# Stores issued by GpSimd, more buffers for divided weights and words, g written into other tiles, and the operands of x made in the order of their products

## The chip, the cores and the metric

The kernel runs on one core of a Trainium2 chip. A core has five engines that run side by side: TensorE (PE, matmuls; PEld is its weight load), VectorE (DVE), ScalarE (ACT), GpSimd (POOL) and SyncE (SP, which here only issues DMAs). Each engine takes its instructions strictly in the order in which the program lists them, and waits on semaphores for the others. The metric is the device time of one execution in microseconds (us), lower is better; the numbers below are for one core and one program.

## What is computed

Attention with a sigmoid in place of the softmax, over 8 batches, 12 heads, 448 tokens and 64 columns a head, then a bilinear feed-forward layer on the 3584 x 768 result:

```
scores = q @ k.T / sqrt(64) - log(448)
x      = concat_heads(sigmoid(scores) @ v)      # 3584 x 768
h      = ((x @ w1) * (x @ w2)) @ w3             # 3584 x 1024
out    = h @ w_out                              # 3584 x 768
```

The four weights are of type float64 and reach the kernel as pairs of 32-bit words. The kernel makes float32 values of them itself ("decode").

## The kernel before, in words

**Precision.** A float32 operand is divided into a high part in the type `fp32r` and the rest, also in that type: `split` casts the high part (`h...`, on ACT or DVE) and lets DVE subtract it (`l...`). A product is three matmuls: high x high, high x low, low x high.

**Products.** `x @ w` is done with Strassen's scheme in Winograd's form: seven products instead of eight. The two batches 2g and 2g+1 are one group g (four groups). For each of the three 128-wide slices kc of x, seven operands are made of the four blocks A11, A12, A21, A22 of x: A11, S2, A12, S3, S1, A22, S4, in the order of the products (`PRODUCTS`). S1 = A21 + A22, S2 = S1 - A11, S3 = A11 - A21, S4 = A12 - S2. `up(g)` runs over the eight 128-wide slices fc of the hidden width and, in each, over the seven products k; a product is 9 matmuls (3 slices kc x 3). After each product ACT (`p`, `c11`) or DVE (`u2`, `u3`, `c22`) takes its sum out of the accumulators; after k = 5 and k = 6 DVE multiplies two of these tiles and the result g goes to DRAM (`g_dram`).

**Weights.** `prepare_weights` decodes w1 and w2 slice by slice (12 steps on DVE for each fc, plus a magnitude on ACT), and `finish_weights` makes the seven weight operands of a slice, divides each of them (`divide`: a cast on ACT, a subtraction on DVE, tile `wo`) and stores it (`w_dram`). `load_weights` fetches them again for each group into a ring of six tiles `w`. `prepare_rest` does the same decoding for w3 and w_out (tiles `raw` and `f`, 32 jobs).

**Order.** All engines follow the order in which the program is written. Attention is a row of 168 items, two to a burst k (84 bursts and one more); a burst issues the scores of its two items, the sigmoids on ACT, and the products with v of the burst before. From burst 25 on, `up(0)` is taken between attention (504 matmuls over bursts 25 to 52, 18 a burst), then `up(1)` (bursts 58 to 66, 56 a burst) and `up(2)` (71 to 79). `up(3)` follows the last burst. After each product `beside` takes steps of other streams: one step of `change` (the operands of x for the next group, from `groups`), else 3 or 4 steps of `weights` in group 0, else 2 steps of `rest`. In bursts without products four steps of `change` and two of `weights` are taken. In group 0 the operands are made in `combine`, as soon as a slice of x is there.

**Queues.** Before the change every DMA is issued by SP, in program order: loads of `qk`, `vv`, `raw` and `w`, and the stores of `wo`, `f` and g. `finish_weights` keeps the stores of two divided weights back (`made`), with three buffers `wo`; `up` keeps the stores of g until the next product.

**The end.** Under the last matmuls of `up(3)` w_out is loaded and split (`woh`, `wol`, eight slices) and the first two slices of w3 (`w3`, `w3h`, `w3l`); then w3 @ w_out (L702) and the last product (L827) follow, which the change does not touch.

Of the kernel before, what the change touches and what calls it, by code (L numbers as in the profile page):

```python
# [25 lines left out]
def sigmoid_attention_bilinear_ffn(  # L26
# [20 lines left out]
    P = 128  # L47
# [168 lines left out]
    def early(g, kc):  # L216

        for name in ("A11", "S3"):
            split_operand(g, name, kc, xf[g, name, kc])
            yield  # L220

    def late(g, kc):

        a11, a12, s1, a22 = (xf.pop((g, name, kc)) for name in ("A11", "A12", "A21", "A22"))
        split_operand(g, "S1", kc, s1)
        yield
        total(a11, s1, a11, ALU.subtract)
        split_operand(g, "S2", kc, a11)
        yield
        if g > 0:  # L230
            split_operand(g, "A12", kc, a12)
            yield
        total(a12, a12, a11, ALU.subtract)
        split_operand(g, "S4", kc, a12)
        yield
        split_operand(g, "A22", kc, a22)
        yield

    def combine(n, acc):
# [53 lines left out]
    def finish_weights(fc, fs):  # L293

        b11, b21, b12, b22 = (f[:, h * KH:(h + 1) * KH] for f in fs for h in range(2))
        made = []
# [7 lines left out]
        def store():  # L304
            k, wo = made.pop(0)
            nc.sync.dma_start(out=w_dram[fc * 7 + k], in_=wo.bitcast(F32))
# [19 lines left out]
        n4 = subtract("n4", b21, t2)  # L326
# [4 lines left out]
        store()  # L331
        yield 1
        store()

    RING = 6
    stored = set()
# [16 lines left out]
            jobs.append((src, wo_dram[ic, :, ms]))  # L353
    def prepare_rest():

        def load(i):
            return load_words(jobs[i][0], p2[0]) if i < len(jobs) else None

        raw = [load(0), load(1)]
        yield  # L360
        yield
        f = magnitude(raw[0], p2[0], 3)
        store = None
        for i, (_, dst) in enumerate(jobs):
            for step, _ in enumerate(decode(raw[i % 2], f)):
                if step == 0 and store:
                    nc.sync.dma_start(out=store[0], in_=store[1])
# [6 lines left out]
        nc.sync.dma_start(out=store[0], in_=store[1])  # L374
        yield

    def up(g):

        at = {b: slice(b * S, (b + 1) * S) for b in (2 * g, 2 * g + 1)}
        stores = []  # L380
        for fc in range(NF):
            tags = ["up0", "up1"] * 2 if g < NG - 1 else ["up0", "up1", "av", "av"]
            if fc % 2 and g < NG - 1:
# [13 lines left out]
            def add(out, a, b):  # L397
                nc.vector.tensor_tensor(out=out, in0=a, in1=b, op=ALU.add)  # L398

            def leave(b, a, out):  # L400
                nc.vector.tensor_tensor(out=out, in0=a, in1=out, op=ALU.mult)
                stores.append((g_dram[fc, :, at[b]], out))

            for k, name in enumerate(PRODUCTS):
                n = (g * NF + fc) * 7 + k
                load_weights(n + RING - 1)
                w = ring.pop(n)
                while any((name, kc) not in ops[g] for kc in range(KH)):
                    next(change)
                for dst, src in stores:  # L410
                    nc.sync.dma_start(out=dst, in_=src)
                stores.clear()
                bank, start, stop = ((0, 1, 0), (1, 1, 0), (0, 0, 1), (1, 0, 1),
                                     (2, 1, 0), (3, 1, 1), (2, 0, 1))[k]
                if start:
                    chain(bank)
                a = acc[bank]
                for kc in range(KH):
                    xh, xl = ops[g][name, kc]
                    for m, (i, x) in enumerate(((0, xh), (0, xl), (1, xh))):  # L420
                        nc.tensor.matmul(  # L421
                            a, w[:, i, kc], x, start=bool(start) and kc == 0 and m == 0,
                            stop=bool(stop) and kc == KH - 1 and m == 2, skip_group_check=True,
                        )
                        if (kc, m) != (KH - 1, 2):
                            yield
# [6 lines left out]
                elif k == 2:  # L433
                    c11 = kept("c11")
                    nc.scalar.copy(out=c11, in_=a)
# [12 lines left out]
                beside(g, n)  # L448
                yield
        for dst, src in stores:  # L450
            nc.sync.dma_start(out=dst, in_=src)

    def take(stream, n):
        done = 0
# [9 lines left out]
    zeros = p1.tile([P, 512], F32R, name="wo", bufs=3)  # L464
    nc.vector.memset(zeros.bitcast(F32), 0.0)

    def idle_products(n):
# [27 lines left out]
    def groups(g):  # L495
        if g < NG - 1:
            for kc in range(KH):
                yield from early(g, kc)
                yield from late(g, kc)
            return  # L500
        for kc in range(KH):
            yield from early(g, kc)
        for kc in range(KH):
            while (g, "A22", kc) not in xf:
                yield
            yield from late(g, kc)

    qks, splits, vvs = {}, {}, {}
    qks[0] = load_pair(0)
# [46 lines left out]
    for k in range(NBURST + 1):  # L556
# [43 lines left out]
    phase_a.close()  # L600
# [261 lines left out]
```

## Time and profile before

| | |
|---|---|
| time, median of 3 runs | 1085.17 us (1083.5 to 1087.89) |
| the profiled execution, its own time | 1085.67 us |
| the profiled execution, span of its trace | 1083.8 us |
| PE busy | 1004.1 us of the span |
| mean granted TensorE clock | 0.962 |
| DVE, ACT busy | 650.3 us, 410.7 us |
| DMA | 226.39 MB, mean 209 GB/s |

Busy times are sums over the span. A row of the waits reads: the waiting engine, its tile and line, who ended the wait; total us, number of waits, the longest. A row of the timeline reads: start, length, engine, line, operation, tiles, and in brackets the idle time before it with what ended it. A row of the stages reads: from:to, length, then busy us and number of instructions of PE, PEld, DVE, ACT and POOL, the granted clock, the DMA engines' busy share and GB/s.

### The profile page before, as it was taken

The page shows a single profiled execution, that of the slowest core. Times are in us where ns is not written, and L with a number is a line of the kernel's source. Part 1 is how long each engine was busy: PE and PEld are TensorE (multiplying, and loading weights), DVE is VectorE, ACT ScalarE, POOL GpSimd, SP SyncE. Part 2 cuts the span into 40 slices and gives each one's busy share as a digit, 9 for nine tenths or more (in the row PEclk, how much of TensorE's full clock was granted, in tenths as well). Part 3 has the DMA queues.
Part 4 walks back from the last instruction along what each step waited for, and adds up shares of the span by engine and source line. Part 5 has one row for each costly group of instructions (what it writes and reads, how often), then busy time and mean ns, then how long its engine had stood idle before and what let it go on. Part 6 is the DMA issues. An engine that isn't in the chain of part 4 may idle for free.

```text
span 1083.8 us, 14159 instructions
## 1 busy us (share of the span) xinstructions
PE 1004.1 (93%) x5250; PEld 766.4 (71%) x5250; DVE 650.3 (60%) x1042; ACT 410.7 (38%) x598; POOL 0.2 (0%) x4
## 2 busy tenths in 40 slices
PE   9976879888999899999799999799989999999998
PEld 4432456555666487777377777499879999999997
DVE  5767456766733966667856674844335565666563
ACT  6855634444553632323523332411114342323130
POOL 0000000000000000000000000000000000000000
PEclk9987989888999999999899999899999999999999
DMA  7554587787975487899387896098834113433402
GB/s 240 195 186 163 200 310 265 282 278 264 329 266 178 125 299 245 300 329 323 102 285 259 309 314 216 17 323 296 287 129 166 55 59 112 161 106 133 135 36 77
DMA packets 122436, 226.39 MB, mean 209 GB/s; under 512 B 10752, under 2 KB 80384, under 8 KB 122368
## 3 DMA queue, kind: packets, MB, share of 16 engines
q1 hardware_dynamic: 122368, 225.49, 61.6%
q8 instruction: 42, 0.69, 0.3%
q14 instruction: 26, 0.21, 0.1%
HBM read 170.39 MB, written 55.05 MB: 208 GB/s over the span
## 4 chain that ended last, share of the span: by engine, by line
PE 50%; DVE 5%; DMA 1%; ACT 1%; issue 1%; SPq 0%; DVEq 0%; ACTq 0%
PE up L421 21%; PE up L827 19%; PE up L702 6%; PE av L189 1%; PE sp L166 1%; DMA w<-w_dram 1%; DVE lS L67 1%; DVE A L214 1%; DVE lA L67 1%; DVE u L398 0%; PE sp L176 0%; DVE hS L66 0%; PE av L197 0%; ACT a L156 0%; DVE low L67 0%
## 5 line engine op out<-in xcount | busy, mean ns | idle before, releaser
L421 PE MATMUL up<-hS,w 128*128 128x448 f32 x768 | 244.2, 377 | 30.0 <-DVE u L398 13.1
L827 PE MATMUL up<-gh,wo 128*128 128x448 f32 x672 | 192.2, 367 | 0.0
L421 PEld LDWEIGHTS up<-hS,w 128*128 128x128 f32 x768 | 146.7, 192 | 64.1 <-DVE u L398 14.6
L156 ACT ACTIVATE a<-sp,bias 128x896 f32<-128x896 f32 x168 | 160.5, 1004 | 75.7 <-PE sp L166 71.5
L421 PE MATMUL up<-hA,w 128*128 128x448 f32 x576 | 183.6, 372 | 3.4 <-ACT p L429 3.2
L421 PE MATMUL up<-lS,w 128*128 128x448 f32 x384 | 143.2, 373 | 0.3 <-DVE lS L67 0.2
L827 PEld LDWEIGHTS up<-gh,wo 128*128 128x128 f32 x672 | 126.1, 188 | 11.3
L189 PE MATMUL av<-a,vv 128*64 128x448 f32 x576 | 132.5, 575 | 0.0
L421 PEld LDWEIGHTS up<-hA,w 128*128 128x128 f32 x576 | 109.5, 190 | 25.5 <-issue 7.8
L827 PE MATMUL up<-gl,wo 128*128 128x448 f32 x336 | 123.2, 367 | 0.0
L421 PE MATMUL up<-lA,w 128*128 128x448 f32 x288 | 106.7, 371 | 0.0
L166 PE MATMUL sp<-high 64*128 64x448 f32 x288 | 65.9, 454 | 37.9 <-ACT a L156 37.8
L398 DVE TENSOR_TENSOR u<-up,p 128x448 f32<-128x448 f32 x64 | 39.9, 623 | 83.5 <-PE up L421 78.6
L166 PEld LDWEIGHTS sp<-high 64*128 64x128 f32 x288 | 28.9, 197 | 85.7 <-ACT a L156 60.4
L189 PEld LDWEIGHTS av<-a,vv 128*64 128x64 f32 x576 | 35.0, 141 | 68.5 <-issue 67.3
L76 ACT ACTIVATE f<-raw 128x768 f32<-128x768 f32 (+2 forms) x48 | 34.5, 720 | 121.1 <-DMA raw<-w3T 43.9
L421 PEld LDWEIGHTS up<-lS,w 128*128 128x128 f32 x384 | 73.8, 192 | 8.3 <-issue 1.4
L827 PEld LDWEIGHTS up<-gl,wo 128*128 128x128 f32 x336 | 63.1, 188 | 5.6
L398 DVE TENSOR_TENSOR u<-up,u 128x448 f32<-128x448 f32 x64 | 39.8, 622 | 42.4 <-PE up L421 41.7
L67 DVE TENSOR_TENSOR low<-qk,high 128x896 fp32r<-128x896 f32 x48 | 52.3, 1090 | 20.2 <-ACT high L66 16.1
L421 PEld LDWEIGHTS up<-lA,w 128*128 128x128 f32 x288 | 54.8, 190 | 7.1 <-issue 2.8
L67 DVE TENSOR_TENSOR gl<-gf,gh 128x896 fp32r<-128x896 f32 x40 | 41.9, 1087 | 29.7 <-ACT gh L66 21.4
(80 smaller groups left out, 1203.1 us busy)
## 6 DMA issues: line engine op xcount, KB each, us to landing
w<-w_dram SPq DMA_DIRECT2D x224, 384.0 KB, 4.9
w_dram<-wo SPq DMA_DIRECT2D x56, 384.0 KB, 5.1
g_dram<-c SPq DMA_DIRECT2D x64, 224.0 KB, 4.0
gf<-g_dram SPq DMA_DIRECT2D x16, 896.0 KB, 5.3
raw<-w SPq DMA_DIRECT2D x16, 768.0 KB, 5.5
qk<-qT SPq DMA_DIRECT2D x48, 224.0 KB, 5.0
qk<-kT SPq DMA_DIRECT2D x48, 224.0 KB, 5.0
out<-o_sb SPq DMA_DIRECT2D x48, 224.0 KB, 2.0
```

The lines of the kernel that those rows point to most:

```text
L67: lo_engine.tensor_tensor(out=dst_lo, in0=src, in1=dst_hi, op=ALU.subtract)
L76: nc.scalar.activation(f, raw[..., 1].bitcast(F32), AF.Abs, scale=HW_SCALE)
L156: nc.scalar.activation(dst, src, AF.Sigmoid, bias=bias[:n], scale=scale)
L166: nc.tensor.matmul(sp[:, j], k[rows, 1, at:at + P], q[rows, 0], start=m == 0, stop=m == 2)
L189: nc.tensor.matmul(acc[cols, :S], vv[:, c, at:at + D], a[:, j], start=u == 0 and c == 0, stop=u == 1 and c == NC - 2,)
L214: nc.vector.tensor_tensor(out=out, in0=in0, in1=in1, op=op)
L398: nc.vector.tensor_tensor(out=out, in0=a, in1=b, op=ALU.add)
L421: nc.tensor.matmul(a, w[:, i, kc], x, start=bool(start) and kc == 0 and m == 0, stop=bool(stop) and kc == KH - 1 and m == 2, skip_group_ch ...
L702: nc.tensor.matmul(acc, a[:, jc], w[:, jc, ms], start=(jc == 0 and m == 0), stop=(jc == NF - 1 and m == 2),)
L827: nc.tensor.matmul(acc, w[:, fc, ms], g[:, fc], start=start and fc == 0 and m == 0, stop=fc == NH - 1 and m == 2, skip_group_check=True,)
```

## The change

Five parts:

1. Every store (`wo`, g, and the `f` of w3 and w_out) is issued by GpSimd at once, no longer by SP and no longer kept back. SP issues loads and the final outputs.
2. `wo` has four buffers instead of three, `raw` in `prepare_rest` four instead of two, with words loaded three jobs ahead; the magnitude of the next job is taken at step 4 instead of 2. The divisions of a slice come in the order 0, 2, 5, 1, 3, 4, 6 instead of 0, 2, 1, 3, 4, 5, 6; n4 is written over b21.
3. g is written into `u3` (k = 5) and into a new tile under the name `c22` (k = 6), instead of into `c22` and `c11`.
4. The operands of x: in group 0 the high parts of S1 to S4 are cast on DVE (all were on ACT), in the other groups those of S2 and S4 (it alternated). `groups` makes them in the order of the products over all slices kc, and a product waits slice by slice. Bursts without products take three steps of `change` instead of four.
5. Before the end, the first seven products of `up(3)` are placed ahead of the closing of the attention pools, and w3's first two slices are loaded before the eight splits of w_out instead of after them.

```diff
-        turn = g > 0 and len(ops[g]) % 2
+        turn = name in (("S1", "S2", "S3", "S4") if g == 0 else ("S2", "S4"))
...
+    def second(g, kc):
+        a11, s1 = xf.pop((g, "A11", kc)), xf[g, "A21", kc]
+        total(a11, s1, a11, ALU.subtract)
+        xf[g, "S2", kc] = a11
+        split_operand(g, "S2", kc, a11)
+
+    def fourth(g, kc):
+        a12 = xf.pop((g, "A12", kc))
+        total(a12, a12, xf.pop((g, "S2", kc)), ALU.subtract)
+        split_operand(g, "S4", kc, a12)
...
-        def divide(k, src):
-            if len(made) > 1:
-                store()
-            wo = p1.tile([P, 2, KH, P], F32R, name="wo", bufs=3)
-            split(wo[:, 0], wo[:, 1], src, nc.scalar.copy, nc.vector)
-            made.append((k, wo))
+        def divide(k, src):
+            wo = p1.tile([P, 2, KH, P], F32R, name="wo", bufs=4)
+            split(wo[:, 0], wo[:, 1], src, nc.scalar.copy, nc.vector)
+            nc.gpsimd.dma_start(out=w_dram[fc * 7 + k], in_=wo.bitcast(F32))
+            stored.add(fc * 7 + k)
...
-        for k, src in ((1, t2), (3, t3), (4, t1), (5, n4), (6, b22)):
+        for k, src in ((5, n4), (1, t2), (3, t3), (4, t1), (6, b22)):
...
-            return load_words(jobs[i][0], p2[0]) if i < len(jobs) else None
+            if i < len(jobs):
+                raw[i] = load_words(jobs[i][0], p2[0], 4)
...
-                if step == 2 and i + 1 < len(jobs):
-                    following = magnitude(raw[(i + 1) % 2], p2[0], 3)
+                if step == 4 and i + 1 < len(jobs):
+                    following = magnitude(raw[i + 1], p2[0], 3)
                 yield
-            store = dst, f
-            raw[i % 2] = load(i + 2)
+            nc.gpsimd.dma_start(out=dst, in_=f)
             f = following
...
-            def leave(b, a, out):
-                nc.vector.tensor_tensor(out=out, in0=a, in1=out, op=ALU.mult)
-                stores.append((g_dram[fc, :, at[b]], out))
+            def leave(b, a, c, out):
+                nc.vector.tensor_tensor(out=out, in0=a, in1=c, op=ALU.mult)
+                nc.gpsimd.dma_start(out=g_dram[fc, :, at[b]], in_=out)
...
-                while any((name, kc) not in ops[g] for kc in range(KH)):
-                    next(change)
...
+                    while (name, kc) not in ops[g]:
+                        next(change)
...
-                    leave(2 * g + 1, u3, c22)
+                    leave(2 * g + 1, u3, c22, u3)
...
-                    leave(2 * g, u2, c11)
+                    leave(2 * g, u2, c11, kept("c22"))
...
             for kc in range(KH):
                 yield from early(g, kc)
-                yield from late(g, kc)
+                split_operand(g, "S1", kc, xf[g, "A21", kc])
+                yield
+                second(g, kc)
+                yield
+            for name in ("A12", "A22"):
+                for kc in range(KH):
+                    split_operand(g, name, kc, xf[g, name, kc])
+                    yield
+            for kc in range(KH):
+                fourth(g, kc)
+                yield
             return
...
-            take(change, 4)
+            take(change, 3)
...
+    take(filler, 7 * KH * 3 - 9)
     take(rest, 10 ** 6)
...
+    load_w3(0)
+    load_w3(1)
     for jc in range(NF):
-        take(filler, 50)
+        take(filler, 42)
...
-    load_w3(0)
-    load_w3(1)
+    take(filler, 20)
     split_w3(0)
```

Three places show how instructions move. The first is the queue of SP around the start of `up(0)`, before the change: `w` are the loads of divided weights for coming products, `wo` the stores of weights just divided.

```order
L344 DMA w<-w_dram 128x768 x5
L306 DMA w_dram<-wo 128x768 x2
L139 DMA vv<-vL 128x3x256
L145 DMA vs<-vL 64x128 x2
L344 DMA w<-w_dram 128x768
L71 DMA raw<-w 128x6x256
L306 DMA w_dram<-wo 128x768 x2
L344 DMA w<-w_dram 128x768
L306 DMA w_dram<-wo 128x768 x2
L344 DMA w<-w_dram 128x768
```

The same place on SP now:

```order
L339 DMA w<-w_dram 128x768 x5
L71 DMA raw<-w 128x6x256
L139 DMA vv<-vL 128x3x256
L145 DMA vs<-vL 64x128 x2
L339 DMA w<-w_dram 128x768 x3
L71 DMA raw<-w 128x6x256
L339 DMA w<-w_dram 128x768
```

And the queue of POOL, which had no DMA before, from its first store on:

```order
L311 DMA w_dram<-wo 128x768 x16
L395 DMA g_dram<-u_1202 128x448
L311 DMA w_dram<-wo 128x768
L395 DMA g_dram<-c_1326 128x448
L311 DMA w_dram<-wo 128x768 x6
```

The stores have left SP's queue, where they stood between the loads, and stand alone on POOL's.

The second place is DVE around burst 18, where the first slice of x of group 0 is complete. Before, S1 (`A_605`), S2 (`A_218`) and S4 (`A_391`) were each formed (L214) and their low parts subtracted (L67) on DVE, with the cast between the two on ACT:

```order
L214 TENSOR_TENSOR A_605<-A_605,A_792 128x448
L67 TENSOR_TENSOR lS_796<-A_605,hS_795 128x448
L214 TENSOR_TENSOR A_218<-A_605,A_218 128x448
L67 TENSOR_TENSOR lS_801<-A_218,hS_800 128x448
L214 TENSOR_TENSOR A_391<-A_391,A_218 128x448
L67 TENSOR_TENSOR lS_806<-A_391,hS_805 128x448
```

Now (the tiles have other numbers):

```order
L214 TENSOR_TENSOR A_606<-A_606,A_792 128x448
L66 CAST hS_795<-A_606 128x448
L67 TENSOR_TENSOR lS_796<-A_606,hS_795 128x448
L214 TENSOR_TENSOR A_218<-A_606,A_218 128x448
L66 CAST hS_800<-A_218 128x448
L67 TENSOR_TENSOR lS_801<-A_218,hS_800 128x448
L214 TENSOR_TENSOR A_392<-A_392,A_218 128x448
L66 CAST hS_805<-A_392 128x448
L67 TENSOR_TENSOR lS_806<-A_392,hS_805 128x448
```

The three casts have joined DVE's queue and left ACT's.

The third place is DVE in the first slice of `up(3)`. Before, nearly all operands stood ahead of the sum of the second product (`u_6116`); these are the last rows ahead of it, and what follows up to the last sum:

```order
L214 TENSOR_TENSOR A_5115<-A_5115,A_4603 128x448
L66 CAST hS_6088<-A_5115 128x448
L67 TENSOR_TENSOR lS_6089<-A_5115,hS_6088 128x448
L398 TENSOR_TENSOR u_6116<-up,p 128x448
L67 TENSOR_TENSOR lA_6119<-A_6071,hA_6118 128x448
L398 TENSOR_TENSOR u_6146<-up,p 128x448
L398 TENSOR_TENSOR c_6160<-up,u_6146 128x448
L398 TENSOR_TENSOR u_6146<-up,u_6146 128x448
L401 TENSOR_TENSOR c_6160<-u_6146,c_6160 128x448
```

Now the rows from the sum of the sixth product (`u_6127`) to the sum of the seventh (`u_6093`):

```order
L391 TENSOR_TENSOR u_6127<-up,u_6127 128x448
L394 TENSOR_TENSOR u_6127<-u_6127,c_6145 128x448
L214 TENSOR_TENSOR A_4623<-A_4623,A_4224 128x448
L66 CAST hS_6167<-A_4623 128x448
L67 TENSOR_TENSOR lS_6168<-A_4623,hS_6167 128x448
L214 TENSOR_TENSOR A_4815<-A_4815,A_4497 128x448
L66 CAST hS_6177<-A_4815 128x448
L67 TENSOR_TENSOR lS_6178<-A_4815,hS_6177 128x448
L214 TENSOR_TENSOR A_5094<-A_5094,A_4580 128x448
L66 CAST hS_6185<-A_5094 128x448
L67 TENSOR_TENSOR lS_6186<-A_5094,hS_6185 128x448
L391 TENSOR_TENSOR u_6093<-up,u_6093 128x448
```

The making of S4, which the seventh product multiplies, has moved from ahead of the second product's sum to behind the sixth product's.

More of the change, by code (lines that the diff above doesn't have):

```diff
@@ L220, in early @@
             yield
+    def second(g, kc):
[7 more added lines that the diff above has]
+        split_operand(g, "S4", kc, a12)
     def late(g, kc):
-        a11, a12, s1, a22 = (xf.pop((g, name, kc)) for name in ("A11", "A12", "A21", "A22"))
-        split_operand(g, "S1", kc, s1)
+        split_operand(g, "S1", kc, xf[g, "A21", kc])
         yield
-        total(a11, s1, a11, ALU.subtract)
-        split_operand(g, "S2", kc, a11)
+        second(g, kc)
         yield
[L230 to L234, printed above, removed]
+        fourth(g, kc)
         yield
-        split_operand(g, "A22", kc, a22)
+        split_operand(g, "A22", kc, xf[g, "A22", kc])
         yield
@@ L295, in finish_weights @@
         b11, b21, b12, b22 = (f[:, h * KH:(h + 1) * KH] for f in fs for h in range(2))
-        made = []
         def subtract(name, in0, in1, out=None):
@@ L325, in finish_weights @@
         yield 1
-        n4 = subtract("n4", b21, t2)
+        n4 = subtract("n4", b21, t2, b21)
         yield 1
-        for k, src in ((1, t2), (3, t3), (4, t1), (5, n4), (6, b22)):
+        for k, src in ((5, n4), (1, t2), (3, t3), (4, t1), (6, b22)):
             divide(k, src)
             yield 1
-        store()
-        yield 1
-        store()
     RING = 6
@@ L354, in prepare_rest @@
     def prepare_rest():
+        raw = {}
         def load(i):
-            return load_words(jobs[i][0], p2[0]) if i < len(jobs) else None
-        raw = [load(0), load(1)]
-        yield
-        yield
+            if i < len(jobs):
+                raw[i] = load_words(jobs[i][0], p2[0], 4)
+        for i in range(3):
+            load(i)
+        for _ in range(6):
+            yield
         f = magnitude(raw[0], p2[0], 3)
-        store = None
         for i, (_, dst) in enumerate(jobs):
-            for step, _ in enumerate(decode(raw[i % 2], f)):
-                if step == 0 and store:
-                    nc.sync.dma_start(out=store[0], in_=store[1])
-                if step == 2 and i + 1 < len(jobs):
-                    following = magnitude(raw[(i + 1) % 2], p2[0], 3)
+            load(i + 3)
+            for step, _ in enumerate(decode(raw.pop(i), f)):
+                if step == 4 and i + 1 < len(jobs):
+                    following = magnitude(raw[i + 1], p2[0], 3)
                 yield
-            store = dst, f
-            raw[i % 2] = load(i + 2)
+            nc.gpsimd.dma_start(out=dst, in_=f)
             f = following
-        nc.sync.dma_start(out=store[0], in_=store[1])
-        yield
     def up(g):
         at = {b: slice(b * S, (b + 1) * S) for b in (2 * g, 2 * g + 1)}
-        stores = []
         for fc in range(NF):
@@ L407, in up @@
                 w = ring.pop(n)
-                while any((name, kc) not in ops[g] for kc in range(KH)):
-                    next(change)
-                for dst, src in stores:
-                    nc.sync.dma_start(out=dst, in_=src)
-                stores.clear()
                 bank, start, stop = ((0, 1, 0), (1, 1, 0), (0, 0, 1), (1, 0, 1),
@@ L443, in up @@
                     add(u3, a, u3)
-                    leave(2 * g + 1, u3, c22)
+                    leave(2 * g + 1, u3, c22, u3)
                 else:
                     add(u2, a, u2)
-                    leave(2 * g, u2, c11)
+                    leave(2 * g, u2, c11, kept("c22"))
                 beside(g, n)
                 yield
-        for dst, src in stores:
-            nc.sync.dma_start(out=dst, in_=src)
     def take(stream, n):
@@ L463, in sigmoid_attention_bilinear_ffn @@
     order.enter_context(tc.manual_schedule(engines=ALL))
-    zeros = p1.tile([P, 512], F32R, name="wo", bufs=3)
+    zeros = p1.tile([P, 512], F32R, name="wo", bufs=4)
     nc.vector.memset(zeros.bitcast(F32), 0.0)
@@ L498, in groups @@
                 yield from early(g, kc)
-                yield from late(g, kc)
+                split_operand(g, "S1", kc, xf[g, "A21", kc])
+                yield
+                second(g, kc)
+                yield
[4 more added lines that the diff above has]
+            for kc in range(KH):
+                fourth(g, kc)
+                yield
             return
@@ L502, in groups @@
             yield from early(g, kc)
+            split_operand(g, "A12", kc, xf[g, "A12", kc])
+            yield
         for kc in range(KH):
@@ L505, in groups @@
                 yield
-            yield from late(g, kc)
+            second(g, kc)
+            yield
+        for name, source in (("S1", "A21"), ("A22", "A22")):
+            for kc in range(KH):
+                split_operand(g, name, kc, xf[g, source, kc])
+                yield
+        for kc in range(KH):
+            fourth(g, kc)
+            yield
     qks, splits, vvs = {}, {}, {}
```

3 lines of the change are left out of this document (removed).

## The prediction

> **What bounds the kernel now.** I read the busy times and the clock first, then what PE and ACT wait for, then the stages.
>
> ```profile
> PE 1004.1 (93%) x5250; PEld 766.4 (71%) x5250; DVE 650.3 (60%) x1042; ACT 410.7 (38%) x598; POOL 0.2 (0%) x4
> PEclk9987989888999999999899999899999999999999
> ...
> PE sp L166 <- ACT a L156: 37.8, 12, 7.1
> PE up L421 <- DVE u L398: 13.1, 3, 5.4
> PE up L421 <- DVE hS L66: 7.4, 2, 5.9
> PE up L421 <- DVE c L398: 5.3, 1, 5.3
> PE up L421 <- ACT c L435: 4.0, 2, 2.4
> PE up L421 <- ACT p L429: 3.2, 2, 1.7
> ...
> ACT wo L66 <- DMA w_dram<-wo: 64.7, 22, 7.4
> ACT f L76 <- DMA raw<-w3T: 43.9, 11, 8.1
> ACT c L435 <- DMA g_dram<-c: 26.7, 9, 5.2
> ```
>
> PE is the engine that sets the end: it is busy 1004.1 of 1083.8 us and idle 80. No row has PE waiting for a transfer; it waits for ACT and DVE, and ACT, which is busy 38% only, waits 64.7 us for stores of `wo` to free a buffer. So the loss starts at the stores. The clock row shows a second loss: it dips where PE idled. Now the stages, with four short stretches as gauges:
>
> ```profile
> 60.00:117.40 57.40, 41.69 (x222) 17.59 (x218) 35.60 (x57) 34.58 (x50) 0.00 (x0) 0.79 0.53 180
> 117.40:308.00 190.60, 164.16 (x866) 108.31 (x866) 121.42 (x196) 90.42 (x136) 0.00 (x0) 0.92 0.81 281
> ...
> 20.00:40.00 20.00, 20.00 (x136) 8.27 (x132) 17.11 (x25) 16.89 (x22) 0.00 (x0) 1.00 0.65 209
> 280.00:300.00 20.00, 20.00 (x116) 14.10 (x114) 14.40 (x26) 10.68 (x16) 0.00 (x0) 1.00 0.87 294
> 360.00:380.00 20.00, 15.31 (x82) 7.85 (x79) 18.36 (x34) 10.62 (x16) 0.00 (x0) 0.91 0.38 112
> 460.00:480.00 20.00, 20.00 (x104) 16.12 (x103) 13.88 (x30) 4.65 (x7) 0.00 (x0) 1.00 0.94 325
> ```
>
> Stage A (60 to 117.4) is attention before `up(0)`. At the pace of 20 to 40 us, 136 matmuls in 20 us, its 222 matmuls take 32.6 us; it lasts 57.4. Stage B (117.4 to 308) is `up(0)` as long as weights are divided. At the undisturbed pace of 280 to 300 us its 866 matmuls take 149.3 us; it lasts 190.6. PE is busy 41.69 and 164.16 us there, 9 and 15 us over the undisturbed times: that is the slow clock after idle, since A has four stretches of idle (the first and last of them are shown below) and B five, 2 to 3 us for each.
>
> **Stage B, stores and buffers (parts 1 and 2): 25 us gained.** One of its five stalls, on SP, ACT and PE (194.41, between the first and the last), the landing time of such a store, and the stage's matmuls of `up` alone:
>
> ```profile
> 186.71 7.46 SPq L306 DMA_DIRECT2D w_dram<-wo  x2
> ...
> 192.72 0.51 ACT L66 CAST wo<-f 128x384 fp32r<-128x384 f32 x1 [7.35 <-DMA w_dram<-wo]
> ...
> 129.63 0.47 PE L421 MATMUL up<-hS,w 128*128 128x448 f32 x1 [2.88 <-DVE u L398]
> ...
> 194.41 0.74 PE L421 MATMUL up<-hS,w 128*128 128x448 f32 x1 [5.42 <-DVE u L398]
> ...
> 258.61 0.74 PE L421 MATMUL up<-hS,w 128*128 128x448 f32 x1 [4.79 <-DVE u L398]
> ...
> w_dram<-wo SPq DMA_DIRECT2D x56, 384.0 KB, 5.1
> ...
> 117.40:308.00 190.60, 90.45 (x396) 0.92 0.81 281
> ```
>
> With three buffers and two stores held back, the cast needs the buffer whose store has only just been issued; ACT stands 7.35 us, the sums behind it are late, PE stands 5.42. Now a store goes at once and the cast needs the buffer of four divisions before. Closest are the fifth, first, third, fourth and sixth operand in a row: from the first to the last of them lie six steps (four of the stream and two decoding steps between), and `beside` takes 3.4 to a product. The 396 matmuls are 44 products, so in a stage of 166 us 3.8 us each: 6.7 us in all. A store takes some 0.6 us for its low part, 0.4 to issue (below), 5.1 to land: 6.1. No wait is left, with little to spare.
>
> What is late next is the transfers. The DMA engines are 0.81 busy over 190.6 us: 154.4 us of work that the change doesn't shrink. An undisturbed PE stands beside a share of 0.94 above (460 to 480), so I take that as within reach: 154.4 / 0.94 = 164 us. I add 2 us for leftover waits: 166, a gain of 25. PE's own floor, 149, is the lower end; without any gain in rate over 0.85 it is 182.
>
> The Trainium skill, "DMA: Bandwidth & Descriptors", section "Issuing engines are not separate DMA queues", says that DMAs from any issuing engine run on the same 16 engines and that a second issuer saves only issue time. By that rule the stage could not go below 154 us; without it, it would be 149. That no share in the quoted stages is above 0.94 agrees with it.
>
> What a DMA costs on POOL no row shows (POOL has four instructions). The nearest rows are SP's own stores:
>
> ```profile
> L306 SPq DMA_DIRECT2D w_dram<-wo x56: 319/382/2951, 47.3 to 305.5; - x56
> ...
> L306 SPq DMA_DIRECT2D w_dram<-wo x11: 319/383/538, 47.3 to 119.6; - x11
> ```
>
> So an issue lies between 0.3 and 3.0 us; I take the median, 0.4. About 45 of the 56 divided weights and 12 tiles of g go out in stage B: 57 issues, 22 us on an idle engine, or 168 us at 3.0, as long as the stage itself. Then the last division would also wait some 2 us in each slice: B at 178. A POOL DMA waits for DVE's low part, and only other stores queue behind it; ACT waits for their buffers, DVE for tiles of g (five products until the next use, 19 us), SP for weights to load. That last wait is covered: 11 stores are out by 120 us, when five weights have been loaded, and stores and products then go at about the same pace (seven a slice). If that cover were gone, each product would wait the 5.1 us landing.
>
> **Stage A, casts moved to DVE and stores (parts 1, 2, 4): 14 us gained.**
>
> ```profile
> 60.24 0.56 ACT L66 CAST hS<-S 128x448 fp32r<-128x448 f32 x1 [1.59 <-DVE S L214]
> ...
> 103.24 0.56 ACT L66 CAST hS<-A 128x448 fp32r<-128x448 f32 x1 [1.23 <-DVE A L214]
> ...
> 65.87 0.74 PE L166 MATMUL sp<-high 64*128 64x448 f32 x2 [4.86 <-ACT a L156]
> 105.64 0.74 PE L166 MATMUL sp<-high 64*128 64x448 f32 x2 [4.13 <-ACT a L156]
> ...
> L66 DVE CAST hS<-A 128x448 fp32r<-128x448 f32 x15 | 5.9, 392 | 0.4
> L67 DVE TENSOR_TENSOR lS<-A,hS 128x448 fp32r<-128x448 f32 x36 | 22.5, 625 | 12.8 <-ACT hS L66 12.3
> L214 DVE TENSOR_TENSOR A<-A,A 128x448 f32<-128x448 f32 x36 | 22.4, 621 | 11.2 <-ACT A L246 10.9
> ```
>
> The first stall (4.86 us) is a store again. The other three (4.13 here) come from casts on ACT that wait for DVE, 1.2 us each, with sigmoids queued behind them. Eleven such casts stand between 60.24 and 103.24. On DVE they cost 11 x 0.392 = 4.3 us: DVE's 35.6 becomes 39.9 us, over PE's 32.6. So DVE becomes the bound here. The most it reaches is 18.36 of 20 us (360 to 380): 39.9 / 0.918 = 43.5 us, a gain of 14. Bounds: 6, if DVE keeps waiting for ACT's and PE's pieces, and 20, if its arrears run into stage B, where it has room (121 of 166).
>
> **The rest: 21 us gained.**
>
> ```profile
> 366.20 0.47 PE L166 MATMUL sp<-high 64*128 64x448 f32 x2 [4.32 <-ACT a L156]
> ...
> 529.26 0.74 PE L166 MATMUL sp<-high 64*128 64x448 f32 x2 [4.02 <-ACT a L156]
> ...
> 697.99 0.74 PE L421 MATMUL up<-hS,w 128*128 128x448 f32 x1 [5.92 <-DVE hS L66]
> ...
> 790.16 0.74 PE L421 MATMUL up<-hS,w 128*128 128x448 f32 x1 [5.32 <-DVE c L398]
> ...
> 785.60 1.04 ACT L66 CAST w3h<-w 128x1024 fp32r<-128x1024 f32 x1 [4.93 <-DMA w<-w_dram]
> ...
> L67 DVE TENSOR_TENSOR w3l<-w,w3h 128x1024 fp32r<-128x1024 f32 x8 | 9.8, 1222 | 12.0 <-ACT w3h L66 11.9
> ...
> 616.91 11.55 PE up L421 x56
> ```
>
> - The waits for `c` and `p` (4.0 + 3.2 us above) come from ACT behind stores of g and loads of `raw`. Earlier stores, other tiles and four buffers end them but for some 0.7: 6.5 gained.
> - 366 and 529: DVE makes 21 steps of operands for a group, in five or four bursts. Three steps a burst instead of four leave, I estimate, 1.5 of 4.32 and of 4.02 us. The steps moved under `up` run beside products of 11.55 x 9 / 56 = 1.86 us; the longest, S4, is 0.62 + 0.39 + 0.62 = 1.63 and hides, but for one place: S4 now stands behind the two sums of the sixth product, so `up(2)` waits 0.62 + 0.62 + 1.63 = 2.9 us at its seventh. The 1.5 us wait for `hS` that `up(2)` has (the other of the two, 7.4 - 5.9) goes. 9.8 us become 5.9: 3.9 gained.
> - 698: S2 is early now, but S4 is late in the same way, and no attention lies beside it: 2.9, then 1.63 less three matmuls of 0.21, twice 1.0, and 1.5 for the last slice of S2 behind the last attention. 6.4 us instead of 5.9: 0.5 lost.
> - 790: the load of w3 goes out some 70 us earlier (356 matmuls at 0.21). Of 5.3 us 0.5 may stay, as two subtractions of 1.2 us now stand in a row ahead of a sum: 4.8 gained.
> - Slow clock after these four stretches, at 2.3 us each (9.1 / 4, stage A): 9; I count 6, as some idle stays.
>
> 6.5 + 3.9 - 0.5 + 4.8 + 6 = 20.7, 21 in round numbers. The bounds are 10 and 28. The end of `up(0)` (308 to 345), L702 and L827 are untouched.
>
> **Sum.** 25 + 14 + 21 = 60 us. Against the execution's own 1085.67 that is 1025.7; the median of the runs lies 0.5 lower: 1025.
>
> **Rivals.** (1) Transfers bind harder: B only reaches 182 us. For it: SP's and POOL's traffic now mix, and 154 us of transfer must fit. Against: 0.94 was reached beside a busy PE. 1085 - 9 - 14 - 21 = 1041. (2) Neither transfers nor DVE bind: B 153, A 38, the rest 27: 1085 - 38 - 19 - 27 = 1001. (3) The waits only change place: ACT waits for `wo` behind POOL and DVE for tiles of g, since no store lands sooner; then stage B and A keep their lengths and of the rest only the 5.3 us before w3 goes: 1080. Against: a wait of four divisions instead of one. (4) Slower: POOL's queue becomes the bound of stage B. Its 57 stores at X us each take 57 X; the other 35 us of gain are eaten when 57 X = 225.6, X = 4.0 us, ten times SP's median. At 4.2 the stage is 239 us: 1085 + 49 - 35 = 1099. For it: nothing shows POOL issuing a DMA, and DVE is busy 60% beside it. Against: SP's longest is 3.0.
>
> The Trainium skill, "SBUF — State Buffer", sections "SBUF: two separate sides" and "A bandwidth-pool intuition that's wrong (but worth ruling out)", says that a DMA issued by GpSimd waits while DVE holds the port both share in its two-port modes, and gives about 3.1 us instead of 0.62 for one beside a copy. By it rival 4's X would be 3.1, B would be 177 us, and the sum 1036, still faster; no row here can show it yet.
>
> **Chances.** Forecast 0.58 (its own range 1010 to 1042), rival 1 0.18, rival 2 0.10, rival 3 0.06, rival 4 0.08. A range from 1006 to 1058 takes in the forecast, rival 1 with the slow POOL issues, and half of rival 2: 0.81. A change within 0.5% is what a measurement of this kernel cannot tell from none. Faster by more: 0.58 + 0.18 + 0.10 + half of rival 3 = 0.89; within: 0.03; slower: 0.08.
>
> **What would show it.** ACT's wait for stores of `wo` falls from 64.7 to under 12 us; stage B has a DMA share of 0.9 or more; stage A has DVE over 0.9 busy; PE waits for `hS` at the seventh products of `up(2)` and `up(3)`, 2.9 us and in pieces; the 5.3 us before w3 is gone. It is wrong if stores on POOL land in over 8 us, if PE comes to wait for `w`, or if stage B's DMA share stays near 0.81 with PE still idle.

## The result, and the profile after the change

| | before | after |
|---|---|---|
| time, median (lowest to highest, runs) | 1085.66 us (1083.5 to 1087.89, 4) | 1012.41 us (1010.67 to 1013.41, 4) |
| the profiled execution, its own time | 1085.67 us | 1012.75 us |
| its span | 1083.8 us | 1010.9 us |
| mean granted TensorE clock | 0.962 | 0.988 |

The ratio is 0.9323, interval 0.93 to 0.9347: 73 us faster. The busy times and the clock row of the page after:

```profile
PE 985.6 (97%) x5250; PEld 757.1 (75%) x5250; DVE 650.0 (64%) x1042; ACT 407.8 (40%) x598; POOL 85.7 (8%) x156
PEclk9998999999999999999999999899999999999999
```

The span is 72.9 us shorter. PE's idle time fell from 79.7 us (1083.8 - 1004.1) to 25.3: 54.4 us. The same 5250 matmuls were busy 18.5 us less: that part is the clock, whose dips have nearly gone. The waits of the kernel after:

```profile
PE up L411 <- DVE hS L66: 5.7, 3, 2.3
PE sp L166 <- ACT a L156: 5.1, 5, 2.6
PE sp L166 <- DVE high L66: 3.3, 2, 2.1
PE sp L176 <- ACT a L156: 3.3, 1, 3.3
...
ACT wo L66 <- DMA w_dram<-wo: 15.4, 8, 3.5
```

ACT's wait for stores of `wo` fell from 64.7 us to 15.4, PE's for ACT's `a` in L166 from 37.8 to 5.1. PE's waits for `u`, `c` and `p` in `up` are gone. Stages A and B, cut at the same matmuls as before (220 of 222, and 866):

```profile
60.00:104.95 44.95, 37.84 (x220) 15.61 (x217) 40.32 (x68) 27.38 (x37) 3.64 (x6) 0.89 0.67 225
104.95:264.70 159.75, 155.34 (x866) 103.15 (x866) 121.53 (x196) 89.73 (x136) 31.54 (x56) 0.99 0.95 339
```

| stage | before | after | gain | of it PE's idle time | of it PE's busy time |
|---|---|---|---|---|---|
| A | 57.40 | 44.95 | 12.4 | 8.6 | 3.9 |
| B | 190.60 | 159.75 | 30.9 | 22.0 | 8.8 |
| rest | 775.8 | 746.2 | 29.6 | 23.6 | 6.0 |

(Idle is a stage's length less PE's busy time in it; the first 60 us are cut alike in both.) What is left of PE's idle time in `up(2)` and `up(3)` is in the timeline:

```profile
485.61 0.47 PE L411 MATMUL up<-hS,w 128*128 128x448 f32 x1 [2.34 <-DVE hS L66]
...
625.45 0.47 PE L411 MATMUL up<-hS,w 128*128 128x448 f32 x1 [0.99 <-DVE hS L66]
...
636.52 0.48 PE L411 MATMUL up<-hS,w 128*128 128x448 f32 x1 [2.34 <-DVE hS L66]
```

And POOL's stores, which no trace had shown before:

```profile
L311 POOL DMA_DIRECT2D w_dram<-wo x56: 539/539/1128, 33.3 to 255.6; - x56
...
DMA to landing us min/median/max: 2.6/6.0/9.1
```

An issue on POOL takes 0.54 us at the median and 1.13 at most. The first kernels ask what in parts 1 and 2 made the gain of stage B, the next ones take the other parts, and the last ones what is left. All ratios are to the kernel before, run beside each kernel on the same chip, where its median was 1084.5 to 1085.7 us; a difference to the change is one between two such sets.

### The profile page after: what moved, and what is told of

The parts are those of the page before. It is cut to its first block, busy times and chain, and to the rows that moved or that the text cites. A ratio compares the mean times of both kernels' runs of the same rounds, so it can differ in the third digit from the quotient of the medians.

```text
span 1010.9 us, 14247 instructions
## 1 busy us (share of the span) xinstructions
PE 985.6 (97%) x5250; PEld 757.1 (75%) x5250; DVE 650.0 (64%) x1042; ACT 407.8 (40%) x598; POOL 85.7 (8%) x156
## 4 chain that ended last, share of the span: by engine, by line
PE 82%; issue 9%; DMA 2%; ACT 2%; DVE 2%; POOL 1%; SPq 0%; POOLq 0%; DVEq 0%; ACTq 0%
PE up L411 38%; PE up L837 20%; PE av L189 8%; PE sp L166 7%; PE up L712 7%; DMA raw<-w 2%; PE av L197 2%; PE sp L176 1%; ACT a L156 1%; POOL w_dram L311 1%; DMA w_dram<-wo 1%; DVE A L214 0%; DVE lS L67 0%; DVE u L391 0%; DVE hS L66 0%
## 5 line engine op out<-in xcount | busy, mean ns | idle before, releaser
L411 PE MATMUL up<-hS,w 128*128 128x448 f32 x768 | 239.9, 372 | 5.7 <-DVE hS L66 5.7
L411 PEld LDWEIGHTS up<-hS,w 128*128 128x128 f32 x768 | 144.3, 189 | 37.2 <-issue 8.5
L391 DVE TENSOR_TENSOR u<-up,p 128x448 f32<-128x448 f32 x64 | 39.9, 623 | 90.9 <-PE up L411 90.9
L419 ACT COPY p<-up 128x448 f32<-128x448 f32 x32 | 17.1, 535 | 148.7 <-PE up L411 119.7
L166 PE MATMUL sp<-high 64*128 64x448 f32 x288 | 62.8, 432 | 8.5 <-ACT a L156 5.1
L166 PEld LDWEIGHTS sp<-high 64*128 64x128 f32 x288 | 27.3, 185 | 54.5 <-ACT a L156 26.1
L67 DVE TENSOR_TENSOR gl<-gf,gh 128x896 fp32r<-128x896 f32 x40 | 41.9, 1086 | 31.7 <-ACT gh L66 31.7
L66 ACT CAST gh<-gf 128x896 fp32r<-128x896 f32 x40 | 35.8, 942 | 60.1 <-PE up L837 50.0
```

The lines of the kernel that those rows point to most:

```text
L66: hi_engine(out=dst_hi, in_=src)
L67: lo_engine.tensor_tensor(out=dst_lo, in0=src, in1=dst_hi, op=ALU.subtract)
L166: nc.tensor.matmul(sp[:, j], k[rows, 1, at:at + P], q[rows, 0], start=m == 0, stop=m == 2)
L411: nc.tensor.matmul(a, w[:, i, kc], x, start=bool(start) and kc == 0 and m == 0, stop=bool(stop) and kc == KH - 1 and m == 2, skip_group_ch ...
L419: nc.scalar.copy(out=p, in_=a)
```

## The experiments: who issues the stores, how many buffers, what bounds stage B

### The changed kernel with its stores on SP

```diff
-            nc.gpsimd.dma_start(out=w_dram[fc * 7 + k], in_=wo.bitcast(F32))
+            nc.sync.dma_start(out=w_dram[fc * 7 + k], in_=wo.bitcast(F32))
...
-            nc.gpsimd.dma_start(out=dst, in_=f)
+            nc.sync.dma_start(out=dst, in_=f)
...
-                nc.gpsimd.dma_start(out=g_dram[fc, :, at[b]], in_=out)
+                nc.sync.dma_start(out=g_dram[fc, :, at[b]], in_=out)
```

> The changed kernel with its three kinds of store issued by SP again, at the same places of the program and at once. Theory 'queue': what gained was the store's own queue; on SP it stands behind loads that wait for PE, and loads behind it wait for DVE's low parts, so ACT's wait for stores of wo grows from 15 us to over 30 and the time to 1020 to 1030 us. Rival 'buffers': issuing at once and the fourth buffer are enough on any queue; 1010 to 1015 us.

Measured: 1009.91 us, ratio 0.9308 (0.9291 to 0.9325). The interval overlaps that of the change. POOL as the issuer brings nothing that can be measured, and theory 'queue' falls: ACT waits for the stores as long as in the change (15.4 us). New are three waits of PE for `w`, 3.5 us in all.

```profile
ACT wo L66 <- DMA w_dram<-wo: 15.5, 9, 5.0
```

The stage B of this kernel (854 matmuls, to the 396th of `up`), and the row of the same stretch in the changed kernel:

```profile
105.50:259.87 154.37, 152.50 (x852) 102.11 (x852) 119.65 (x194) 88.61 (x134) 0.00 (x0) 1.00 0.99 354
```

```profile
104.95:263.05 158.10, 153.69 (x854) 102.48 (x852) 120.30 (x194) 89.45 (x135) 31.54 (x56) 0.99 0.95 339
```

With the stores on SP the DMA engines are busy 0.99 of the stage and move 354 GB/s beside a PE that is idle for 1.9 us. The ceiling of 0.94 that the prediction took from its best stage was not a ceiling.

### Three buffers again, and the change's transfers made lighter

Three buffers `wo` in the changed kernel:

```diff
-            wo = p1.tile([P, 2, KH, P], F32R, name="wo", bufs=4)
+            wo = p1.tile([P, 2, KH, P], F32R, name="wo", bufs=3)
```

> The changed kernel with three buffers wo instead of four. Theory: divisions in a row lie 1.5 steps (1.6 us) apart, so with three buffers a cast waits for a store begun 4.8 us before that takes about 7 us to low part, issue and landing: two waits of 2 us a slice more, ACT's wait 15 to 40 us, time 1016 to 1024 us. Rival: issue at once is what counts, the fourth buffer nothing; 1010 to 1015 us.

Measured: 1017.49 us, ratio 0.939 (0.9366 to 0.9414), 5 us slower than the change. Its stage B is 163.8 us at a share of 0.92, and the wait comes back in part:

```profile
ACT wo L66 <- DMA w_dram<-wo: 28.4, 16, 3.8
```

In the second, group 0 loads only the high half of each divided weight, and its third matmul takes the high half again. So the low part of the weights is left out of group 0:

```diff
-            nc.sync.dma_start(out=ring[n].bitcast(F32), in_=w_dram[n % (NF * 7)])
+            if n < NF * 7:
+                nc.sync.dma_start(out=ring[n][:, 0].bitcast(F32), in_=w_dram[n, :, 0])
+            else:
+                nc.sync.dma_start(out=ring[n].bitcast(F32), in_=w_dram[n % (NF * 7)])
...
-                            a, w[:, i, kc], x, start=bool(start) and kc == 0 and m == 0,
+                            a, w[:, i if g > 0 else 0, kc], x, start=bool(start) and kc == 0 and m == 0,
```

> The changed kernel where group 0 loads only the high half of each divided weight and its third matmul uses the high half again: same matmuls, 11 MB less to load in up(0), so the DMA share of stage B falls from 0.95 to about 0.80. Theory of the prediction (transfers bound stage B): the stage falls from 160 to 151 to 154 us, the time to 1004 to 1007 us. Rival (PE bounds it, with the few waits for stores that are left): the stage stays within 2 us, 1009 to 1013 us.

Measured: 1005.16 us, ratio 0.9268 (0.9252 to 0.9284). Stage B:

```profile
105.36:257.32 151.96, 151.96 (x854) 102.17 (x852) 119.96 (x194) 89.17 (x135) 31.52 (x56) 1.00 0.87 297
```

PE is busy for the whole of it: 152.0 us is PE's own floor. The changed kernel lies 6.1 us above it, the kernel with SP's stores 2.4 us. So the transfers are what stands last between stage B and this floor, though not as loads that PE waits for: no row of the changed kernel has PE waiting for `w`. With the lighter loads a store of `wo` lands 4.0 us after its issue instead of 6.0, and ACT's wait for these stores is 7.1 us instead of 15.4.

### The kernel before with one half of the idea each

Three kernels made from the kernel before: stores of `wo` at once on POOL and four buffers; stores at once on SP with three buffers; four buffers alone, with two stores still held back on SP. The fourth buffer finds room by writing n4 over b21, which needs the division of n4 first. The first of them; the others are its two halves:

```diff
-            if len(made) > 1:
-                store()
-            wo = p1.tile([P, 2, KH, P], F32R, name="wo", bufs=3)
+            wo = p1.tile([P, 2, KH, P], F32R, name="wo", bufs=4)
             split(wo[:, 0], wo[:, 1], src, nc.scalar.copy, nc.vector)
-            made.append((k, wo))
+            nc.gpsimd.dma_start(out=w_dram[fc * 7 + k], in_=wo.bitcast(F32))
+            stored.add(fc * 7 + k)
...
-        n4 = subtract("n4", b21, t2)
+        n4 = subtract("n4", b21, t2, b21)
-        for k, src in ((1, t2), (3, t3), (4, t1), (5, n4), (6, b22)):
+        for k, src in ((5, n4), (1, t2), (3, t3), (4, t1), (6, b22)):
```

> The kernel before with one thing changed: stores of divided weights go to POOL at once, with four buffers wo (n4 over b21 and the operand order that this needs). Theory: all of stage B's gain and the first stall of stage A, 36 to 40 us: 1046 to 1050 us. Rival: the stores of g, still on SP, hold the loads and the rest back, so stage B gains under 20 us: over 1060 us.

> The kernel before with one thing changed: a divided weight's store goes out at once, on SP, with the three buffers it had. Theory: holding the stores back was the larger part of the loss; stage B falls from 188 to 160 to 166 us and the first stall of stage A goes, 1046 to 1056 us. Rival: the fourth buffer is needed; stage B stays over 175 us, 1068 us or more.

> The kernel before with the fourth buffer wo alone (n4 over b21 and the operand order that this needs), stores still held back by two on SP. Theory: a cast now needs the store issued two divisions before, some 3 us, of the 6 that a store takes: about half of the waits stay, stage B 168 to 176 us, 1062 to 1073 us. Rival: buffers alone are enough, stage B 160 us or less, 1050 us.

| kernel before with | time, us | ratio | stage A | stage B (854) |
|---|---|---|---|---|
| nothing changed | 1085.6 | 1 | 57.4 | 187.7 |
| both, on POOL | 1047.36 | 0.9658 (0.9636 to 0.968) | 49.3 | 156.9 |
| at once, on SP, three buffers | 1054.98 | 0.971 (0.9669 to 0.9751) | 48.9 | 162.3 |
| four buffers alone | 1048.05 | 0.9657 (0.9619 to 0.9694) | 52.9 | 154.9 |

The fourth buffer alone, 37 us below the kernel before, does as much as both together; it came out well below what I had expected of it. Its wait, and that of stores at once with three buffers:

```profile
ACT wo L66 <- DMA w_dram<-wo: 13.4, 10, 2.6
```

```profile
ACT wo L66 <- DMA w_dram<-wo: 24.1, 13, 4.2
```

With three buffers and two stores held back, a cast needs the buffer whose store has just been issued; with four it needs one issued a division earlier. That is enough: 64.7 us of waits become 13.4. Stores at once with three buffers leave 24.1. Either half takes most of the wait, so their gains don't add. The new order of the divisions came with the fourth buffer and was not tried without it in the kernel that holds its stores back.

## The experiments: operands, g, w3

### The operands alone, in the kernel before

The fourth part of the change alone, with the seven early products of the fifth:

```diff
-        turn = g > 0 and len(ops[g]) % 2
+        turn = name in (("S1", "S2", "S3", "S4") if g == 0 else ("S2", "S4"))
...
-            take(change, 4)
+            take(change, 3)
...
+    take(filler, 7 * KH * 3 - 9)
     take(rest, 10 ** 6)
```

> The kernel before with part 4 alone (casts of S on DVE in group 0, operands in the order of the products, three steps a burst, seven products ahead of the closing). Theory: stage A loses its three stalls by casts but DVE bounds it, 8 to 10 us; behind stage B the idle of operands falls from 15.7 to about 6.5 us and slow clock with it, 14 us: 1060 to 1065 us. Rival: the casts and steps only move DVE's load to another place, under 8 us in all: 1077 us or more.

Measured: 1064.95 us, ratio 0.9814 (0.977 to 0.9858), 20.6 us faster than before, or 15 to 25 us by the interval. In its profiled execution (1060.18 us, the fastest of the four) stage A is 52.5 us and B 185.0; the larger part, 18 us of span, lies behind B. The row that went, in the waits of before:

```profile
ACT hS L66 <- DVE A L214: 34.5, 17, 5.4
```

and where it hurt, in ACT's timeline of before:

```profile
364.68 0.56 ACT L66 CAST hS<-A 128x448 fp32r<-128x448 f32 x1 [5.40 <-DVE A L214]
365.15 1.90 ACT L156 ACTIVATE a<-sp,bias 128x896 f32<-128x896 f32 x2
```

The cast stands ahead of two sigmoids and waits 5.40 us for a sum that DVE reaches late; PE's 4.32 us at 366 us follow. With the casts of S2 and S4 on DVE the row isn't in the waits any more, and PE's waits of 4.32 and 4.02 us are gone already in this kernel.

### Four steps of operands a burst again

```diff
-            take(change, 3)
+            take(change, 4)
```

> The changed kernel with four steps of operands instead of three in the bursts without products. Theory: the two waits of PE in these bursts (4.32 and 4.02 us before, gone after) come back, with the slow clock behind them, 4 to 9 us; as more of the operands are then done early, less is left for the seventh products, which gives back up to 3 us: 1014 to 1021 us. Rival: the waits had gone for another reason (DVE casts instead of ACT's): 1008 to 1013 us, with no wait over 1.5 us around 330 to 370 and 480 to 520 us.

Measured: 1008.26 us, ratio 0.9294 (0.9277 to 0.9311). My theory fell: the waits in the bursts before `up(1)` and `up(2)` did not return. The two stretches of this kernel:

```profile
310.00:330.00 20.00, 19.14 (x121) 10.06 (x120) 19.59 (x36) 17.18 (x27) 0.00 (x0) 1.00 0.55 158
470.00:490.00 20.00, 20.00 (x112) 13.96 (x109) 18.13 (x32) 10.64 (x18) 0.54 (x1) 1.00 0.61 186
```

DVE is busy up to 19.59 of 20 us and PE still loses under 1 us. So it was not the number of steps that had made PE wait there. What is left is the cast on ACT that stood in front of the sigmoids, as the timeline of before has it; the new order of the operands came in the same edit and was not tried apart from it. Three steps instead of four gained nothing that these runs show.

### g over its old tiles

```diff
-                    leave(2 * g + 1, u3, c22, u3)
+                    leave(2 * g + 1, u3, c22, c22)
...
-                    leave(2 * g, u2, c11, kept("c22"))
+                    leave(2 * g, u2, c11, c11)
```

> The changed kernel with g written over c22 and c11 again, as before the change (stores still at once on POOL). Theory: the next products' sums wait for the store of g again, but the store now goes at once, so that ACT's wait for the store of c comes back only in part: 0 to 3 us slower than the change, 1012 to 1016 us. Rival A: the other tiles were what took the 6.5 us of waits for c and p away: 1017 to 1020 us, with PE waiting for ACT's c by 3 us or more. Rival B: no wait of ACT for g's store over 1 us, and the time of the change, 1011 to 1013 us.

Measured: 1018.02 us, ratio 0.9392 (0.9368 to 0.9416), 5.6 us slower than the change, as rival A has it:

```profile
ACT c L425 <- DMA g_dram<-c: 43.1, 11, 5.8
...
PE up L411 <- ACT c L425: 5.1, 4, 1.8
```

That the store goes at once doesn't spare ACT the wait: without the other tiles it is 43.1 us, more than the 26.7 before. With them it is gone.

### w3 loaded late again

```diff
-    load_w3(0)
-    load_w3(1)
     for jc in range(NF):
-        take(filler, 42)
+        take(filler, 43)
...
-    take(filler, 20)
+    load_w3(0)
+    load_w3(1)
     split_w3(0)
```

> The changed kernel with w3's first slices loaded where they were before, behind the splits of w_out. Theory: PE's stall of 5.3 us ahead of w3 @ w_out comes back with its slow clock, 2 us: 1018 to 1021 us. Rival: the stall came from the order on DVE, which stays changed: 1011 to 1014 us.

Measured: 1020.05 us, ratio 0.9401 (0.9366 to 0.9436), 7.6 us slower than the change. PE's wait of 5.95 us is back, and the clock after it is low:

```profile
725.74 0.74 PE L411 MATMUL up<-hS,w 128*128 128x448 f32 x1 [5.95 <-DVE c L391]
```

```profile
725.00:735.00 10.00, 9.27 (x33) 8.40 (x34) 3.81 (x7) 0.53 (x1) 1.09 (x2) 0.68 0.53 171
```

## The experiments: what is left

Two steps of operands beside each product instead of one, with the stores on POOL as in the change, and the same with the stores on SP:

```diff
-        if not take(change, 1):
+        if not take(change, 2):
```

> The changed kernel with two steps of the next group's operands beside each product instead of one, stores on POOL as in the change. Theory: 5.7 us of waits for hS and some 2 us of slow clock go: 1004 to 1008 us. Rival: the sums are late instead, 1011 to 1015 us. Beside the same edit with stores on SP it should be 0 to 4 us slower if POOL's later stores cost stage B what the first experiment showed (158.1 against 154.4 us), and equal if that was scatter.

> The changed kernel with all stores on SP's queue (still at once, same buffers) and two steps of the next group's operands beside each product instead of one. Theory: the waits for hS at the seventh products of up(2) and up(3) (5.7 us of idle time in the trace after) and some 2 us of slow clock behind them go, and the sums that come later behind more operand steps cost 0 to 2 us: 1002 to 1006 us, PE's wait for hS under 1.5 us in all. Rival: the steps taken earlier push DVE's sums back, and PE waits for u or c instead: 1008 to 1013 us with PE waiting for DVE's sums by 4 us or more.

Measured: 1004.89 us, ratio 0.9264 (0.9246 to 0.9281), on POOL; 1006.47 us, ratio 0.9275 (0.9254 to 0.9295), on SP. With each other they agree, so the issuer makes no difference here either. Beside the kernel with one step and the same issuer the gain is 7.5 us on POOL, with intervals apart, and 3.4 us on SP, where they overlap (0.9254 to 0.9295 here, 0.9291 to 0.9325 with one step). One way in which a gain comes about is seen in the 10 us around the seventh product of `up(3)`, in the changed kernel and in that with two steps on POOL, and for the latter also in PE's timeline:

```profile
636.00:646.00 10.00, 9.29 (x26) 6.77 (x27) 5.42 (x11) 0.53 (x1) 1.12 (x2) 0.66 0.55 164
```

```profile
632.00:642.00 10.00, 9.24 (x45) 8.31 (x46) 5.20 (x10) 1.81 (x3) 1.08 (x2) 1.00 0.76 248
```

```profile
632.76 0.47 PE L411 MATMUL up<-hS,w 128*128 128x448 f32 x1 [1.14 <-DVE c L391]
```

PE is equally busy in both stretches, but does 26 matmuls in the one and 45 in the other. After the idle 2.34 us the granted clock is 0.66; after the 1.14 us with two steps it is 1.00. At the pace of the second row, 9.24 / 45 = 0.205 us, the 26 matmuls take 5.3 us instead of 9.3: the slow clock cost 4.0 us, more than the wait itself. Over the whole span PE is busy 979.6 us with two steps, 985.6 with one; that is 6.0 of the 6.2 us by which the spans differ. PE's idle time is the same in both, 25.1 and 25.3 us. Of the 5.7 us of waits for `hS` 1.0 is left, but PE now waits 3.6 us for `c` and `u`, and in stage A one wait is longer, 5.16 us instead of 2.63:

```profile
96.87 0.74 PE L166 MATMUL sp<-high 64*128 64x448 f32 x2 [5.16 <-ACT a L156]
```

This last one is not the work of the second step: the wait is 5.16 us as well in the profile of one step with stores on SP, and 2.63 in that of two steps on SP.

That the clock is the gain is not shown either. The same wait of 2.34 us at the seventh product of `up(2)` was followed by a clock of 0.83 in the change (484 to 494 us), and by full clock in the kernel with its stores on SP:

```profile
483.50 0.47 PE L411 MATMUL up<-hS,w 128*128 128x448 f32 x1 [2.34 <-DVE hS L66]
```

```profile
482.00:492.00 10.00, 8.30 (x47) 5.75 (x48) 8.57 (x16) 3.54 (x5) 0.00 (x0) 1.00 0.50 168
```

That kernel has all three waits for `hS`, 5.7 us, and PE busy 980.4 us, as little as with two steps. So the place was right and the gain on POOL is clear, but how much of it the slow clock behind these waits would have cost differs from one profile to the next.

## Why the prediction was right, and where its terms were off

It gave 60 us where 73 came, with stage A 14 (12.4 measured), B 25 (30.9) and the rest 21 (29.6). The measured 1012.4 us lies about midway between the forecast of 1025 and rival 2's 1001: stage A came as forecast, the rest as in rival 2, B between them. Two of the signs were narrowly missed: ACT's wait for stores of `wo` is 15.4 us instead of under 12, and DVE's share in stage A 0.897 instead of over 0.9.

**Stage A** went as worked out: DVE was the bound, with 40.32 us busy (39.9 forecast) in 44.95 us, a share of 0.897 instead of 0.918. Of PE's waits there, 4.3 us name DVE's `high` and `low`, and one of 2.6 us ACT's `a`. The store stall went with the fourth buffer alone (57.4 to 52.9 us) and the cast stalls with the operands alone (52.5).

**Stage B.** The chain from stores to ACT to sums to PE was right, and so was what comes next, the transfers. The mis-sized term is the time that they need. The step "154.4 / 0.94 = 164 us" took the best share of a stage of before for a ceiling; that stage simply had no more to move. The shares measured are 0.95 with stores on POOL and 0.99 on SP. In the changed kernel this is the smaller part: at 0.95 the 154.4 us would still have taken 162.5. The engines were also busy for less than the 154.4 us, 0.95 x 159.75 = 151.8, with the same 54 MB moved (281 GB/s over 190.6 us, 339 over 159.75), and the 2 us of leftover waits did not come on top. PE's own floor was put too low: with half the loads of group 0 left out, the 866 matmuls take 153.4 us with PE busy throughout, not 149. The kernels with full loads end 2 us (SP) to 6 us (POOL) above this floor, on the cut of 854 matmuls. The step "a store goes at once and the cast needs the buffer of four divisions before" was right but had two causes for one effect: the buffer alone suffices. "No wait is left" was not: 15.4 us in 8 waits stayed, and one of them, in the changed kernel's timeline on ACT and on PE, is the one long wait left in stage B:

```profile
159.17 0.51 ACT L66 CAST wo<-f 128x384 fp32r<-128x384 f32 x1 [3.49 <-DMA w_dram<-wo]
...
161.48 0.98 PE L176 MATMUL sp<-qk 64*64 64x448 f32 x8 [3.25 <-ACT a L156]
```

**POOL's issue** was taken as 0.4 us and is 0.54; 57 issues are 31 us (31.54 measured in B) on an engine that waits for DVE anyway. So the rival in which POOL becomes the bound was far from its 4.0 us. The landing, 5.1 us on SP before, is 6.0 on POOL, but 6.2 with the same stores at once on SP: it is not POOL that makes it longer. Lighter loads shorten it (4.0 us on POOL with half the loads of group 0); what else sets it is open, as stores at once on SP with three buffers landed in 5.0 us. The Trainium skill, "SBUF — State Buffer", section "A bandwidth-pool intuition that's wrong (but worth ruling out)", warns of about 3.1 us for a DMA of GpSimd's beside a copy on DVE; with DVE 0.76 busy in stage B (121.53 of 159.75 us) POOL's longest issue was 1.13 us, so the stores of `wo` do not show it. The stores of g landed later on POOL than on SP (last section); no run shows whether for this reason.

**The rest.** Slow clock was counted as 6, and PE's busy time fell by 6.0; that these agree is in part luck, since more of the idle time went than was counted. The idle time was mis-sized: 14.7 forecast (6.5 + 3.9 - 0.5 + 4.8), 23.6 measured. The waits for `c` and `p` went in full (7.2 for 6.5), w3's too (5.3 for 4.8). "Three steps a burst instead of four leave 1.5 us of 4.32 and of 4.02" was wrong in its reason: both went wholly, with four steps as with three. No cast on ACT waits for DVE's sum any more; I had seen that same stall in stage A and had not looked for it behind the other two. The wait at the seventh products came as forecast, 2.34 + 0.19 us in `up(2)` for 2.9; in `up(3)` 0.99 for the 1.5 of S2's last slice and 2.34 + 0.18 for 2.9, while the two pieces of 1.0 at S4's later slices did not show: 3.5 us for 6.4.

The parts measured singly are the fourth buffer with its order 37.5, the operands with the early products 20.6, w3 7.6, and the tiles of g 5.6 us: 71.3 of 73.2. The first two were added to the kernel before and the other two taken out of the changed one, so the sum is only a rough account. Four buffers `raw` and the later magnitude were not tried alone. ACT's waits for words of w3 and w_out, 43.9 and 37.7 us before, are gone after the change; what that is worth in time is open. So is why stage B is some 3 us longer with the stores on POOL in each pair (158.1 to 154.4, 156.9 to 153.2), while the times agree.

## What to carry to other kernels

When an engine with little work holds up the one that bounds, look at how old the store is whose buffer it needs: one more buffer did as much here as stores at once, and a second queue for them did nothing that could be measured. A conversion that waits for a slower engine should not stand in the queue that also feeds PE. Price an idle stretch of PE with the slow clock that may stand behind it, and don't take the highest share of a busy resource in a trace for its ceiling when nothing shows that it was the limit there.

## What the runs showed of the hardware

- With the stores on SP and two steps, stage B ran at the end of what the DMA engines gave, 153 us of mixed loads and stores at a share of 1.00, beside a PE that was idle for 1.1 us:

```profile
105.83:259.03 153.20, 152.09 (x852) 102.28 (x852) 120.03 (x194) 88.97 (x134) 0.00 (x0) 1.00 1.00 359
```

- How long PE idles decides only in part whether its clock falls. In the fourteen profiles of this case all 46 waits of 3 us or more were followed by a granted clock of 0.50 to 0.72 over the next 3 us, and all 30 waits of 0.94 to 1.16 us by 1.00. Between them both occur: 2.34 us were followed by 0.66 (change, 636 to 646 us) and by 1.00 (stores on SP, 482 to 492 us). The Trainium skill, "TensorE: Matmul & The Clock Gate", section "What's actually happening", has the clock fall after an idle window of about 3.4 us; in this case 2.34 us were at times enough, and the measurement decides.
- A store of g of 224 KB landed 4.8 us after its issue on POOL (median of 64, first view) and 2.7 us on SP (second view), with the same kernel otherwise; with two steps it was 4.5 and 3.0. Why is open:

```profile
L395 POOL DMA_DIRECT2D g_dram<-u x32: 539/540/677, 125.1 to 733.5; - x32
...
DMA to landing us min/median/max: 2.2/4.8/7.9
```

```profile
L395 SPq DMA_DIRECT2D g_dram<-u x32: 319/320/496, 126.5 to 729.4; - x32
...
DMA to landing us min/median/max: 1.9/2.7/7.3
```
